# A rarely taken general path behind a fused transformer block: fewer engines in its conditional, another order of its blocks

## The chip, the cores and the metric

The kernel runs on one core of a Trainium2 chip. A core has five engines with an instruction queue each: TensorE (matrix products, written to PSUM), VectorE, ScalarE, GpSimd and SyncE; in the profile's lines they are PE (with PEld for its weight loads), DVE, ACT, POOL and SP. A letter q behind a name means the engine's queue itself (a branch, a semaphore, a DMA issue) and not its compute. Sixteen DMA engines move data between the chip's main memory and SBUF; they also bring the engines' instructions. Engines wait for each other by semaphores. The metric is the device time of one execution in microseconds (us); the time of a kernel is the median of its runs.

## The reference

One transformer block with conditioning: 2048 tokens of 512 values, 32 heads of 16, a gated feed-forward part of width 1376, inputs and output in bfloat16.

```python
mod = silu(c) @ w_mod                       # six vectors: sa, ca, ga, sb, cb, gb
h = layernorm(x) * (1 + ca) + sa
q, k, v = split(h @ wqkv)                   # 32 heads of 16
phi(y) = concat(softmax(y @ w_phi), softmax(-(y @ w_phi)))
kv = sum over tokens of phi(k)^T v;  z = sum over tokens of phi(k)
o = (phi(q) @ kv) / (phi(q) @ z + 1e-6)
x = x + ga * (o @ wo)
h = layernorm(x) * (1 + cb) + sb
x = x + gb * ((sigmoid(h @ w_gate) * (h @ w_up)) @ w_down)
```

The softmax runs over the 16 features of one head. Its maximum needs to be subtracted only where the exponent could overflow.

## The kernel before

**Tiling.** The 2048 tokens are 16 tiles of 128. For each tile the first part normalises, transposes and scales the input (`h1T`), multiplies it by the folded weights `wqk_f` (w_phi is multiplied into wqkv once at the start), takes the exponentials without subtracting a maximum, and sums `kvacc` over all tiles. The second part, `downstream`, works through the tiles in chunks of 1, 1, 2, 4, 4 and 4: queries, quotient, output projection, second normalisation, gate and up products (`g_ps`, `u_ps`, lines 854 to 859), gated product (lines 864 to 875), and the down product `y_ps` (line 895). A final addition on VectorE (line 905) makes the output tile `ot`, and SyncE stores it (line 907). The last chunk's last two tiles are stored in an order of their own, one of them in two halves of 256 columns, so that the very last store is 64 KB.

**Order.** All this work is entered as tasks in a graph `G` with durations, due times and buffers; a planner puts the tasks in an order, `emit` writes them out, and each engine runs its instructions in that order.

**Two paths.** Leaving out the maximum is safe only where the features are bounded. `bound_tasks` computes such a bound from the weights during the second part and writes `flag`, which is 0 when the bound holds. `load_flag` (lines 913 to 915) reads it into a register of each engine; it is called while the final addition of tile 12 is written out. After all tasks of `G`, line 1306 opens a conditional: if the flag is above 0, a second graph `G2` recomputes everything in the general way, with maxima and minima subtracted, and stores all 16 tiles again. With the inputs used here the flag is 0.

```python
with tc.If(fv_box[0] > 0, preferred_fallthrough_block=False):
    emit(order2)
```

Every engine whose register holds the flag has a test of its own at that place, and a skip part for when the general path doesn't run: it waits until the engine's own earlier work is done and adds to its semaphores what the general path would have added. Loads and stores go through eight semaphores, which SyncE issues DMAs on in turn, so SyncE's skip part has eight such instructions. With `preferred_fallthrough_block=False` the instructions behind the test are the skip part, and the general path is elsewhere.

**The closing.** At the end of the program (line 1333) SyncE waits for all semaphores, the five engines drain and report to GpSimd, GpSimd clears the semaphores, and a second round of reports ends the execution.

**What `G2` uses.** `features` computes the products on TensorE, maxima, minima, differences, sums, reciprocals and products on VectorE, and exponentials on ScalarE; the rest of `G2` is the same `downstream` as in the first graph, with VectorE for most of the element-wise work and SyncE for transposes and for 17 stores.

Of the kernel before, what the change touches and what calls it, by code (L numbers as in the profile page):

```python
# [9 lines left out]
FP32 = mybir.dt.float32  # L10
BF16 = mybir.dt.bfloat16
INT32 = mybir.dt.int32
ACT = mybir.ActivationFunctionType
ALU = mybir.AluOpType
AX = mybir.AxisListType

P = 128
S, D, H, DH, F = 2048, 512, 32, 16, 1376
NT = S // P
KT = D // P  # L20
FT = (F + P - 1) // P
F_LAST = F - (FT - 1) * P
NG = 8
VC = DH + 1
# [402 lines left out]
def kernel(  # L427
# [4 lines left out]
    nc = tc.nc  # L432
    pe, act, dve, pool, sp = nc.tensor, nc.scalar, nc.vector, nc.gpsimd, nc.sync

    ctx.enter_context(tc.manual_schedule())
    cst = ctx.enter_context(tc.tile_pool(name="cst", bufs=1))
    psp = ctx.enter_context(tc.tile_pool(name="psp", bufs=1, space=bass.MemoryType.PSUM))


    x_sb = cst.tile([P, NT, D], BF16, name="x_sb")  # L440
    wv_sb = cst.tile([P, KT, D], BF16, name="wv_sb")
    wqk_f = cst.tile([P, KT, 2 * D], BF16, name="wqk_f")
    wo_sb = cst.tile([P, KT, D], BF16, name="wo_sb")
    wg_sb = cst.tile([P, KT, F], BF16, name="wg_sb")
    wu_sb = cst.tile([P, KT, F], BF16, name="wu_sb")
    wd_sb = cst.tile([P, FT, D], BF16, name="wd_sb")
    wr_sb = cst.tile([P, KT, P], BF16, name="wr_sb")
    h1T = cst.tile([P, KT, S], BF16, name="h1T")
    kvbd = cst.tile([P, NG, P + 16], BF16, name="kvbd")
    ident = cst.tile([P, P], BF16, name="ident")  # L450
    bmask = cst.tile([P, P], BF16, name="bmask")
    mask4 = cst.tile([P, 4], BF16, name="mask4")
    modc = cst.tile([P, 16], FP32, name="modc")
    mhalf = cst.tile([P, NT], FP32, name="mhalf")
# [14 lines left out]
    flag = cst.tile([1, 1], INT32, name="flag")  # L469
# [14 lines left out]
    VS = 4  # L484
    vaug = [cst.tile([P, H, VC], BF16, name=f"vaug{i}") for i in range(VS)]
# [3 lines left out]
    o_v = out.flatten_outer_dims().rearrange("(n p) d -> p n d", p=P)  # L489
    wqkv_v = A_wqkv.rearrange("(j p) n -> p j n", p=P)  # L490
    wmod_v = w_mod.rearrange("(j p) n -> p j n", p=P)
    bm = bmask[:].rearrange("p (h f) -> p h f", f=DH)
# [19 lines left out]
    CAPS = {"bank": 8, "r2k": 6, "xn": 8, "x1": 9, "eT": 3, "h2": 2, "hm": 2, "tg": 2, "ot": 2, "smS": 2, "m": 2, "den": 2, "cc": 3, "ks": 3, "oT": 3, "vaug": VS}  # L512
# [13 lines left out]
    def bank(name, shape=None, dtype=FP32):  # L526
        return Buf("bank", shape or [P, 512], dtype, name)

    def small(name, shape):
        return Buf(name if name in CAPS else "ks", shape, FP32, name)  # L530

    def emit(order):
        for t in order:
            for b in t.bufs:
                if b.cls not in ("h2", "hm", "vaug"):
                    get(b)
            t.fn(t.eng)
# [4 lines left out]
    def kv_tasks(G, acc, t, ph, va, due, parts=((0, 8),), chain=()):  # L542
        for a, b in parts:
            def kv(e, a=a, b=b):
                for g in range(a, b):
                    pe.matmul(acc[g // 4][:, (g % 4) * HC:(g % 4 + 1) * HC], lhsT=ph[:, g * P:(g + 1) * P],  # L546
                              rhs=vaug[va.slot][:, 4 * g:4 * g + 4, :].rearrange("p h d -> p (h d)"),
                              start=(t == 0 and g % 4 == 0), stop=(t == NT - 1), skip_group_check=True)
            halves = [("kvacc", h) for h in range(2) if a < 4 * h + 4 and b > 4 * h]
            G.add(f"kv{t}.{a}", {"PE": 0.031 * (b - a)}, kv, r=[("phi", t, a), ("vaug", t)], w=[*halves, *chain],  # L550
                  bufs=[ph, va] + [acc[h] for _, h in halves], due=due)
# [359 lines left out]
    fv_box = []  # L911

    def load_flag():
        fv_box.append(nc.values_load(flag[0:1, 0:1], min_val=0, max_val=1,
                                     skip_runtime_bounds_check_because="written as 0 or 1"))

    def bound_tasks(G, due):
        for j in range(KT):
# [150 lines left out]
    for g, ts in enumerate(LG):  # L1069
        n = len(ts)  # L1070
        gd = T0 + ts[0] * KP + LGD[g]
# [17 lines left out]
        if nmr_used:  # L1089
            def f_nm(e, ts=ts):  # L1090
                for t in ts:
                    dve.tensor_scalar(nmr[:, 0, t:t + 1], mv1[:, t, 0:1], rs1[:, t:t + 1], -1.0, op0=ALU.mult, op1=ALU.mult)
            G.add(f"nmr1_{g}", {"DVE": 0.02 + 0.1 * n}, f_nm,
                  r=[("rs1", g)], w=[("nmr1", g)], due=gd)
        for t in ts:
            xn = Buf("xn", [P, D], BF16, "xn")
            xns.append(xn)

            def f_xn(e, t=t, xn=xn):
# [4 lines left out]
                else:  # L1104
# [3 lines left out]
                  bufs=[xn], due=gd, port=("POOL", "DVE"), pref=XN1[t] if t < 2 else [e for e in XN1[t] if e != "DVE"] or ["ACT"])  # L1108
        if TD[g]:
            for q, t in enumerate(ts):  # L1110
                G.add(f"xT1_{t}", {"SP": 1.22}, lambda e, t=t, xn=xns[q]: sp.dma_start_transpose(h1T[:, :, t * P:(t + 1) * P], xn[:]),
                      r=[("xn1", t)], w=[("h1raw", t)], bufs=[xns[q]], due=gd, nbytes=-1)
        for j in range(KT):
            dst = h1T[:, j, ts[0] * P:(ts[-1] + 1) * P]
# [24 lines left out]
    for t in range(NT):  # L1139
# [8 lines left out]
        def f_v(e, t=t, vp=vp):  # L1148
            for j in range(KT):
                pe.matmul(vp[:], lhsT=h1T[:, j, t * P:(t + 1) * P], rhs=wv_sb[:, j, :], start=(j == 0), stop=(j == KT - 1))  # L1150
# [6 lines left out]
        for a, b in parts:  # L1157
# [12 lines left out]
            w = (b - a) / 8.0  # L1170
# [65 lines left out]
    order = G.order()  # L1236
    emit(order)

    G2 = Graph(CAPS)

    def features(t, side, key):
        sv = "p (h s j) -> p s h j" if side else "p (s h j) -> p s h j"

        pk = bank("pk_g")

        def f1(e):
            for j in range(KT):
                pe.matmul(pk[:], lhsT=h1T[:, j, t * P:(t + 1) * P], rhs=wqk_f[:, j, side * D:(side + 1) * D], start=(j == 0), stop=(j == KT - 1))
        G2.add(f"gp{side}{t}", {"PE": 0.9}, f1, w=[("gp", side, t), "chain"], bufs=[pk])
        ext = small("ext", [P, 2, H])  # L1250
        dd = [Buf("r2k", [P, H, DH], FP32, "dd") for _ in range(2)]
        ph = Buf("r2k", [P, 2 * H * DH], BF16, "gphi")

        def f2(e):
            pv = pk[:].rearrange("p (h j) -> p h j", j=DH)
            dve.tensor_reduce(ext[:, 0], pv, axis=AX.X, op=ALU.max)
            dve.tensor_reduce(ext[:, 1], pv, axis=AX.X, op=ALU.min)
            for s in range(2):
                dve.tensor_tensor(dd[s][:], pv, ext[:, s].unsqueeze(2).to_broadcast([P, H, DH]), op=ALU.subtract)

        def f3(e):
            for s in range(2):
                act.activation(dd[s][:], dd[s][:], ACT.Exp, scale=1.0 - 2.0 * s)

        def f4(e):
            for s in range(2):
                dve.tensor_reduce(ext[:, s], dd[s][:], axis=AX.X, op=ALU.add)
            dve.reciprocal(ext[:], ext[:])
            for s in range(2):
                dve.tensor_tensor(ph[:].rearrange(sv, s=2, j=DH)[:, s], dd[s][:],  # L1270
                                  ext[:, s].unsqueeze(2).to_broadcast([P, H, DH]), op=ALU.mult)
        G2.add(f"gd{side}{t}", {"DVE": 2.8}, f2, r=[("gp", side, t)], w=[("gd", side, t), "chain"], bufs=[pk, ext] + dd + [ph])
        G2.add(f"ge{side}{t}", {"ACT": 1.2}, f3, r=[("gd", side, t)], w=[("ge", side, t), "chain"], bufs=dd)
        G2.add(f"gn{side}{t}", {"DVE": 2.8}, f4, r=[("ge", side, t)], w=[key, "chain"], bufs=[ext] + dd + [ph])
        return ph

    acc = [bank(f"gacc{i}") for i in range(2)]
    for t in range(NT):
        ph = features(t, 1, ("phi", t, 0))
        vp = bank("gv")  # L1280
        va = Buf("vaug", None, None, "gva")

        def f_v(e, t=t, vp=vp):
            for j in range(KT):
                pe.matmul(vp[:], lhsT=h1T[:, j, t * P:(t + 1) * P], rhs=wv_sb[:, j, :], start=(j == 0), stop=(j == KT - 1))
        G2.add(f"gV{t}", {"PE": 0.9}, f_v, w=[("v", t), "chain"], bufs=[vp], due=t)
        G2.add(f"gva{t}", {"ACT": 0.6}, lambda e, vp=vp, va=va: act.copy(vaug[va.slot][:, :, 0:DH], vp[:].rearrange("p (h d) -> p h d", d=DH)),
               r=[("v", t)], w=[("vaug", t), "chain"], bufs=[vp, va], due=t)
        kv_tasks(G2, acc, t, ph, va, t, chain=["chain"])
    kvbd_tasks(G2, acc)  # L1290
    eT2 = [Buf("eT", [P, NG, 512], BF16, f"geT{cq}") for cq in range(4)]
    for cq in range(4):
        for tl in range(4):
            t = 4 * cq + tl
            ph = features(t, 0, ("gphq", t))
            tp = bank("gtp", [P, NG, P], BF16)

            def f_t(e, ph=ph, tp=tp):
                for g in range(NG):
                    pe.transpose(tp[:, g, :], ph[:, g * P:(g + 1) * P], ident[:])  # L1300
            G2.add(f"gT{t}", {"PE": 0.5}, f_t, r=[("gphq", t)], w=[("gT", t), "chain"], bufs=[ph, tp], due=100.0 + t)
            G2.add(f"gTc{t}", {"ACT": 1.0}, lambda e, cq=cq, tl=tl, tp=tp: act.copy(eT2[cq][:, :, tl * P:(tl + 1) * P], tp[:]),
                   r=[("gT", t)], w=[("eT", cq, tl)], bufs=[tp, eT2[cq]], due=100.0 + t)
    downstream(G2, eT2, 200.0, False)
    order2 = G2.order()
    with tc.If(fv_box[0] > 0, preferred_fallthrough_block=False):
        emit(order2)


# [28 lines left out]
```

## Time and profile before

| what | us |
|---|---|
| median of three runs | 216.68 (216.2 to 217.49) |
| span of the profiled execution, first to last instruction | 215.3 |
| time of that execution itself | not listed beside its span |
| TensorE busy | 202.7 |
| VectorE busy | 166.1 |
| ScalarE busy | 113.0 |
| GpSimd busy | 101.3 |
| last matmul, end | 209.3 |
| last store, issue | 209.7 |

The profile comes from one execution; its times count from the first instruction. The page's table of engines counts compute only: branches, register loads, semaphores, drains and DMA issues are not in it and are seen by asking for their lines. The conditional is line 1306, the flag's loads are line 914, the closing is line 1333. In the DMA table the queue q1 carries the kernel's transfers and the queues q8 and q14, of the kind "instruction", carry instructions: q8 packets of 16 KB, q14 packets of 8 KB. A DMA share is a part of all 16 engines, so one engine at work is a share of 0.06.

### The profile page before, as it was taken

How to read it: one execution, taken by the hardware profiler on the slowest of the kernel's cores; microseconds unless marked ns; L12 is line 12 of the kernel's file. 1: busy time of each engine (PE TensorE's matmuls, PEld its weight loads, DVE VectorE, ACT ScalarE, POOL GpSimd, SP SyncE). 2: the span in 40 equal slices, each digit the busy share in tenths (PEclk: the TensorE clock that was granted, in tenths of full speed). 3: DMA queues.
4: the chain of work that ended last, by engine and by line, in shares of the span. 5: the costliest groups of instructions: out<-in, count | busy, mean ns of one | idle time of the engine just before them, and what ended most of it. 6: DMA issues, size and time to landing. Idle time of an engine off the chain costs nothing.

```text
span 215.3 us, 4319 instructions
## 1 busy us (share of the span) xinstructions
PE 202.7 (94%) x1512; PEld 113.4 (53%) x1539; DVE 166.1 (77%) x447; ACT 113.0 (53%) x278; POOL 101.3 (47%) x133
## 2 busy tenths in 40 slices
PE   7998998999999999989999999999999999999980
PEld 2744454555666577857964544454444444444450
DVE  3799999988689999859989978999899871237340
ACT  3699987998959894345442233643211651235000
POOL 3859999999969999511552222403205210000000
PEclk9999999999999999999999999999999999999996
DMA  6997997970000210250614110233201231000111
GB/s 183 371 255 167 372 193 164 411 246 0 0 3 0 52 26 5 59 90 1 99 24 72 27 28 7 68 73 74 52 14 37 52 73 50 0 0 0 55 50 34
DMA packets 31423, 18.76 MB, mean 87 GB/s; under 512 B 20673, under 2 KB 29346, under 8 KB 31394
## 3 DMA queue, kind: packets, MB, share of 16 engines
q1 hardware_dynamic: 30864, 18.39, 33.2%
q8 instruction: 14, 0.23, 0.4%
q14 instruction: 15, 0.12, 0.2%
q10 hardware_dynamic: 530, 0.02, 0.1%
HBM read 11.58 MB, written 2.10 MB: 64 GB/s over the span
## 4 chain that ended last, share of the span: by engine, by line
PE 70%; DVE 9%; DMA 8%; SPq 4%; issue 2%; ACT 2%; POOL 1%; DVEq 0%; POOLq 0%
PE y_ps L895 16%; PE u_ps L854 15%; PE g_ps L854 15%; PE a_ps L762 5%; PE v_ps L1150 4%; DMA wqk_sb<-in_A_wqkv_dram 4%; PE k_ps L1146 3%; PE q_ps L1224 3%; SPq L1044 3%; DVE u L735 2%; DMA oT<-o 2%; DMA x_sb<-in_A_x_dram 2%; PE num L645 2%; PE kvacc L546 2%; PE g_ps L856 1%
## 5 line engine op out<-in xcount | busy, mean ns | idle before, releaser
L864 ACT ACTIVATE tg<-g_ps 128x512 bf16<-128x512 f32 (+4 forms) x66 | 28.9, 453 | 57.7 <-PE g_ps L854 43.8
L875 DVE SCALAR_TENSOR_TENSOR wmod_sb<-tg,u_ps 128x512 bf16<-128x512 bf16 (+4 forms) x63 | 29.7, 494 | 17.3 <-PE u_ps L854 9.4
L895 PE MATMUL y_ps<-wd_sb,wmod_sb 128*128 128x512 bf16 (+3 forms) x178 | 41.3, 366 | 0.4
L753 POOL TENSOR_TENSOR o<-u 128x512 bf16<-128x512 f32 x14 | 17.7, 1268 | 32.0 <-DVE u L720 15.0
L1168 POOL TENSOR_TENSOR phi<-e,ks 128x1024 bf16<-128x1024 bf16 (+2 forms) x22 | 31.4, 1454 | 0.5 <-DVE ks L1178 0.3
L854 PEld LDWEIGHTS <-wg_sb 128*128 128x128 bf16 (+1 forms) x252 | 21.6, 99 | 16.2 <-issue 1.0
L854 PEld LDWEIGHTS <-wu_sb 128*128 128x128 bf16 (+1 forms) x252 | 21.8, 99 | 15.2
L895 PEld LDWEIGHTS <-wmod_sb 128*128 128x128 bf16 (+1 forms) x187 | 17.9, 98 | 16.4
L854 PE MATMUL u_ps<-wT_sb,wu_sb 128*128 128x512 bf16 (+2 forms) x123 | 23.3, 322 | 0.2
L854 PE MATMUL g_ps<-wT_sb,wg_sb 128*128 128x512 bf16 (+2 forms) x121 | 23.2, 321 | 0.1
L854 PE MATMUL g_ps<-wqk_sb,wg_sb 128*128 128x128 bf16 (+4 forms) x127 | 19.8, 287 | 0.5 <-DVE wqk_sb L828 0.4
L1165 DVE TENSOR_REDUCE ks<-e 128x64 f32<-128x1024 bf16 (+2 forms) x22 | 19.7, 906 | 0.6 <-ACT e L1162 0.6
L854 PE MATMUL u_ps<-wqk_sb,wu_sb 128*128 128x128 bf16 (+4 forms) x127 | 19.6, 287 | 0.1
L905 DVE TENSOR_TENSOR ot<-y_ps,x 128x512 bf16<-128x512 f32 (+1 forms) x17 | 11.2, 656 | 9.8 <-PE y_ps L895 9.8
L1162 ACT ACTIVATE e<-k_ps 128x512 bf16<-128x512 f32 (+2 forms) x44 | 18.3, 499 | 0.3 <-POOL phi L1168 0.3
L762 PE MATMUL a_ps<-wo_sb,oT 128*128 128x512 bf16 x62 | 16.3, 379 | 1.2 <-DMA oT<-o 1.0
L1229 ACT ACTIVATE eT<-q_ps 128x512 bf16<-128x512 f32 x32 | 16.8, 618 | 0.9 <-PE q_ps L1224 0.9
L1146 PE MATMUL k_ps<-wqk_f,h1T 128*128 128x512 bf16 x60 | 15.9, 379 | 1.1 <-ACT h1T L1126 0.8
L1150 PE MATMUL v_ps<-wv_sb,h1T 128*128 128x512 bf16 x63 | 15.8, 379 | 0.1
L1224 PE MATMUL q_ps<-h1T,wqk_f 128*128 128x512 bf16 x60 | 15.1, 378 | 0.1
L1075 DVE BATCH_NORM_STATS2 st<-x_sb 128x6 f32<-128x512 bf16 x16 | 10.8, 676 | 3.3 <-DMA x_sb<-in_A_x_dram 3.3
L767 DVE TENSOR_TENSOR x<-a_ps,x_sb 128x512 f32<-128x512 f32 x16 | 10.9, 684 | 2.5 <-PE a_ps L762 2.3
(154 smaller groups left out, 322.3 us busy)
## 6 DMA issues: line engine op xcount, KB each, us to landing
wmod_sb<-in_w_mod_dram SPq DMA_DIRECT2D x4, 512.0 KB, 6.5
out_dram<-ot SPq DMA_DIRECT2D x15, 128.0 KB, 1.7
x_sb<-in_A_x_dram SPq DMA_DIRECT2D x3, 512.0 KB, 7.5
wg_sb<-in_B_w_gate_dram SPq DMA_DIRECT2D x1, 1376.0 KB
wu_sb<-in_B_w_up_dram SPq DMA_DIRECT2D x1, 1376.0 KB, 9.4
wd_sb<-in_B_w_down_dram SPq DMA_DIRECT2D x1, 1280.0 KB, 12.2
wqk_sb<-in_A_wqkv_dram SPq DMA_DIRECT2D x2, 512.0 KB, 4.3
wmod_sb<-in_w_mod_dram SPq DMA_DIRECT2D x1, 1024.0 KB, 8.3
```

The lines of the kernel that those rows point to most:

```text
L753: G.add(f"o{t}", {"POOL": 1.3, "DVE": 0.62}, lambda e, ub=ub, o=o: engine(e).tensor_tensor(o[:], ub[0][:].rearrange("p h d -> p (h d)"), u ...
L762: pe.matmul(ap_[:], lhsT=oT[:, j, :], rhs=wo_sb[:, j, :], start=(j == 0), stop=(j == KT - 1))
L854: pe.matmul(ps[:fsz, 0:n], lhsT=w[:, j, ft * P:ft * P + fsz], rhs=h[:, j, 0:n], start=(j == 0), stop=(j == KT - 1))
L864: G.add(f"tg{k}.{ft}", {"ACT": 0.13 + n * 0.00083}, lambda e, tg=tg, g_ps=g_ps, fsz=fsz, n=n: act.activation(tg[:fsz, 0:n], g_ps[:fsz, 0:n ...
L875: dve.scalar_tensor_tensor(hm_all[:fsz, hm[k].slot, ft, 0:n], tg[:fsz, 0:n], 1.0, u_ps[:fsz, 0:n], op0=ALU.add, op1=ALU.mult)
L895: pe.matmul(y[:, 0:c1 - c0], lhsT=hm_all[:fsz, hm[k].slot, ft, tl * P:(tl + 1) * P], rhs=wd_sb[:fsz, ft, c0:c1], start=(ft == 0), stop=(ft ...
L1146: pe.matmul(kp[:], lhsT=h1T[:, j, t * P:(t + 1) * P], rhs=wqk_f[:, j, D:2 * D], start=(j == 0), stop=(j == KT - 1))
L1150: pe.matmul(vp[:], lhsT=h1T[:, j, t * P:(t + 1) * P], rhs=wv_sb[:, j, :], start=(j == 0), stop=(j == KT - 1))
L1162: act.activation(ee[:, ha:hb, s, :], kp[:, ha * DH:hb * DH].rearrange("p (h j) -> p h j", j=DH), ACT.Exp, scale=1.0 - 2.0 * s)
L1165: dve.tensor_reduce(ks[:, ha:hb].rearrange("p h s -> p (h s)"), ee[:, ha:hb].rearrange("p h s j -> p (h s) j"), axis=AX.X, op=ALU.add)
L1168: pool.tensor_tensor(ph[:, ha * 32:hb * 32].rearrange("p (h j) -> p h j", j=DH), ee[:, ha:hb].rearrange("p h s j -> p (h s) j"), ks[:, ha: ...
L1224: pe.matmul(qp[:], lhsT=wqk_f[:, j, blk * P:(blk + 1) * P], rhs=h1T[:, j, cq * 512:(cq + 1) * 512], start=(j == 0), stop=(j == KT - 1))
```

## The change

Three things change, and nothing in the tasks of the graph `G`.

1. The flag is loaded on TensorE, ScalarE and GpSimd only. VectorE and SyncE have no register with it and no conditional.
2. The general path is written anew, tile by tile, without a graph, for these three engines. What VectorE did goes to GpSimd: maxima, minima and sums by halving (`gen_fold`), reciprocals by a power (`gen_recip`), products and additions; ScalarE copies every PSUM result to SBUF first. Transposes are done by TensorE (`gen_transposed`). The results are gathered in `x_sb`, and one DMA, issued by GpSimd, stores all of them.
3. The conditional is opened without `preferred_fallthrough_block`.

```diff
     def load_flag():
-        fv_box.append(nc.values_load(flag[0:1, 0:1], min_val=0, max_val=1,
-                                     skip_runtime_bounds_check_because="written as 0 or 1"))
+        fv_box.append(nc.values_load(flag[0:1, 0:1], engines=[mybir.EngineType.PE, mybir.EngineType.Activation, mybir.EngineType.Pool],
+                                     min_val=0, max_val=1, skip_runtime_bounds_check_because="written as 0 or 1"))
...
-    G2 = Graph(CAPS)
-
-    def features(t, side, key):
...
+    def gen_fold(src, n, op, name):
+
+
+        r = src.shape[1]
+        t, d = gen_tile("r2k5", [P, r, n // 2], FP32, name), None
+        if op != ALU.add:
+            d = gen_tile("r2k4", [P, r, n // 2], FP32, name + "d")
+        while n > 1:
+            n //= 2
+            a, b = src[:, :, 0:n], src[:, :, n:2 * n]
+            if op == ALU.add:
+                pool.tensor_tensor(t[:, :, 0:n], a, b, op=ALU.add)
...
+    def gen_features(t, side):
+        pk = gen_bank(0)
+        for j in range(KT):
+            pe.matmul(pk[:], lhsT=h1T[:, j, t * P:(t + 1) * P], rhs=wqk_f[:, j, side * D:(side + 1) * D], start=(j == 0), stop=(j == KT - 1))
+        ps = gen_tile("x10", [P, H, DH], FP32, "g_pk")
+        act.copy(ps[:].rearrange("p h d -> p (h d)"), pk[:])
...
+    def gen_keys():
+        acc = [gen_bank(1 + i) for i in range(3)]
+        for t in range(NT):
+            ph = gen_features(t, 1)
...
+    def gen_tokens(t):
+        ph = gen_features(t, 0)
+        tp = gen_transposed(ph, NG, 1, "g_tp")
...
+        yo = gen_tile("x11", [P, D], FP32, "g_y")
+        act.copy(yo[:], y[:])
+        pool.tensor_tensor(x_sb[:, t, :], yo[:], x1[:], op=ALU.add)
...
-    downstream(G2, eT2, 200.0, False)
-    order2 = G2.order()
-    with tc.If(fv_box[0] > 0, preferred_fallthrough_block=False):
-        emit(order2)
+    with tc.If(fv_box[0] > 0):
+        gen_keys()
+        for t in range(NT):
+            gen_tokens(t)
+        pool.dma_start(o_v[:, :, :], x_sb[:])
```

## The prediction

> **What bounds the kernel now.** I read three things in order: the chain that ended last, to see where the compute stops; the instructions of the lines of the conditional and of the closing, which the page of busy engines leaves out; and the DMA after the last store.
>
> The chain over the last 20 us, with its start, its length and what it was:
>
> ```profile
> 198.63 5.19 PE y_ps L895 x24
> 203.81 0.05 issue
> 203.87 5.40 PE y_ps L895 x35
> 209.27 0.02 issue
> 209.29 0.42 DVE ot L905
> ```
>
> TensorE sets the pace up to 209.3, then one addition on VectorE ends at 209.71. The span is 215.3, so 5.6 us (2.6%) lie behind the last computed value. The general path does not run in this execution, since behind the conditional (line 1306) nothing follows but the closing (line 1333). What the queues do meanwhile, by line: instruction, count, duration in ns (min/median/max), first and last start.
>
> ```profile
> L1306 SPq EVENT_SEMAPHORE  x8: 17/17/17, 212.8 to 213.3; - x8
> L1306 ACTq COMPARE_BRANCH  x2: 38/44/49, 198.7 to 199.0; - x2
> L1306 PEldq COMPARE_BRANCH  x2: 95/1890/3686, 206.4 to 209.4; - x2
> L1306 DVEq COMPARE_BRANCH  x2: 51/53/55, 209.3 to 209.9; - x2
> L1306 SPq COMPARE_BRANCH  x2: 43/48/53, 210.1 to 213.4; - x2
> ...
> L1333 SPq EVENT_SEMAPHORE  x10: 17/28/28, 213.9 to 215.2; - x10
> L1333 ACTq DRAIN  x2: 8/44/80, 201.4 to 214.8; - x2
> L1333 DVEq DRAIN  x2: 10/34/58, 212.7 to 214.8; - x2
> L1333 PEldq DRAIN  x2: 8/40/73, 213.2 to 214.8; - x2
> ```
>
> Each engine has two branches: the test, not taken here, and a jump over the general path, which lies behind. TensorE's jump at 209.4 takes 3.69 us; ScalarE's closing begins 2.4 us after its jump at 199.0, VectorE's 2.8 us after its jump at 209.9. SyncE tests at 210.1, and its next instruction starts only at 212.8. These waits show whom it stood for, the first being the last store's landing:
>
> ```profile
> SPq L1306 <- SPq L1306: 2.7, 1, 2.7
> SPq L1333 <- PEq L1333: 0.6, 2, 0.5
> ```
>
> Why that landing is so late is in the DMA. First the stores' time from issue to landing; then four stretches behind the last issue (start:end, length, engines, granted clock, DMA share, GB/s); then the queues between 210.5 and 211.78:
>
> ```profile
> DMA to landing us min/median/max: 1.5/1.7/2.9
> ```
> ```profile
> 209.70:211.00 1.30, 0.00 (x0) 0.00 (x0) 0.02 (x1) 0.00 (x0) 0.00 (x0) 1.00 0.49 157
> 211.00:211.75 0.75, 0.00 (x0) 0.00 (x0) 0.00 (x0) 0.00 (x0) 0.00 (x0) 0.92 0.00 0
> 211.75:212.25 0.50, 0.00 (x0) 0.00 (x0) 0.00 (x0) 0.00 (x0) 0.00 (x0) 0.50 0.07 8
> ```
> ```profile
> q1 hardware_dynamic: 136, 0.06, 16.7%
> q8 instruction: 1, 0.02, 5.1%
> q14 instruction: 1, 0.01, 1.5%
> ```
>
> The last store is issued at 209.74 and its data moves by 211.0, except one sixteenth (a share of 0.07 of 16 engines) which moves between 211.75 and 212.25, after a pause. In the pause the one 16 KB instruction packet of q8 is in flight: it starts at 210.73 and takes 1.05 us, 1.3 us behind TensorE's jump. So I read it as TensorE fetching its jump target through the DMA engine that also carries that sixteenth. The landing comes at 212.81; 15 of its 16 parts had landed by 211.44.
>
> **The change, part by part.** The sum goes against this execution. Its span is 215.26 us; no other time of its own is listed. The median of the three runs, 216.68, is 1.42 above the span, and I keep those 1.42 for what lies around it.
>
> *Loads of the flag on VectorE and SyncE go.* They took 0.54 and 0.51 us at 200.2 and 201.3. VectorE's lies beside the addition of 200.18 to 200.87, SyncE's between two stores of which the second waits for data until 202.81. Gain 0; without that cover each would give its half microsecond once. The other three loads stay in place, TensorE's 0.49 us at 199.8 under matmuls without a gap.
>
> *VectorE's conditional goes:* two branches, one semaphore, 2.8 us up to its closing at 212.7. SyncE reached its own end only at 214.44, so this alone gives 0.
>
> *SyncE's conditional goes.* Behind the landing at 212.82 stand eight semaphore instructions (0.6 us), then a branch, and the closing's first wait is at 213.92: 1.10 us, all on the path. Nothing replaces it on SyncE, since the new general path issues nothing there. The gain is 1.10; it cannot be negative by any row, and it is at most that plus the closing's own eight waits (0.5 us, 213.92 to 214.44) should those have passed before the landing. I take 1.10, because the closing as it stands waits for this store's semaphore first.
>
> *The block order.* Before, the skip runs straight on, waits until its engine has done its own work and then jumps far. In the default order I expect the general path to follow the test and the skip to be the jump. TensorE's test is at 206.4, 2.9 us before its last matmul ends. If the far jump is taken there, its 3.69 us end at 210.1, and its closing starts about 210.3 rather than 213.2. The fetch, 1.3 us behind the jump, would occupy its DMA engine from 207.7 to 208.75. Stores there: the one issued at 206.16 has landed by 207.68, and the next, issued at 208.81, moves data from 209.64. So the last store lands in its undisturbed time, 209.74 plus 1.5 to 1.7, 211.25 to 211.45; I take 211.4, so 1.41 earlier than 212.81. At worst the gain is 0 (the jump stays behind the last matmul); no row gives more than 1.55. TensorE's next fetch came 4.6 us after the jump (214.04), which would now be 211.0, just behind the store's last packet at 210.93: close enough to matter below. VectorE's own small fetch at 210.87 disappears as well.
>
> *What is queued behind the jump:* on TensorE only its semaphore and the closing; 13 or so matmuls are before it and should already be queued. Nobody waits for that engine's closing before 212. ScalarE's jump (198.7) and GpSimd's (177.2) have 10 us and more of room; at 2.4 us each they hide.
>
> *The general path's new body and its one store on GpSimd's DMA.* It does not run, so its instructions cost nothing. What exists on the skip side is GpSimd's bookkeeping for a DMA that did not go: one more semaphore instruction (17 ns) at 177.3, hidden. In the closing one more wait may join SyncE's eight, 0.06 us. What a DMA queue of GpSimd costs a launch, the trace does not show. From below 0; from above the dearest thing on a queue other than TensorE's, ScalarE's 2.4 us between jump and closing. I take 0.06, the semaphore rows being nearest to what is added.
>
> Sum: landing 211.4, then the closing as before, 215.26 - 213.92 = 1.34, gives 212.75; with 0.06 still 212.8. That is 2.5 us less: 216.68 - 2.5 = 214.2.
>
> **The rivals.**
>
> *The jump stays late.* If a taken branch waits for the matmuls before it, or if the default order is the one there is, TensorE's fetch again lies over the last store. All taken branches in this trace stand behind their engine's own wait, so nothing shows one with work in flight; the tests not taken do run ahead (206.4, against the last matmul's end at 209.3). The same holds if the second fetch slides 0.1 us earlier into the store. Landing 212.81 + 1.34 = 214.15 (TensorE's closing at 213.2 still comes in time), a gain of 1.1: 215.6.
>
> *GpSimd's queue eats the gain.* With 2.4 us added behind the landing the span is 212.75 + 2.4 = 215.15: 216.6, no change. Against it: GpSimd's closing now consists of instructions of 0.03 to 0.14 us.
>
> *TensorE fetches twice (the slower side).* If the skip part and the closing lie too far apart, two far jumps follow each other. Place: behind the last matmul; price: a second 3.69 us. First jump 209.44 to 213.13, second to 216.8, then 0.1 of draining and 0.75 of the final barrier: 217.7, so 219.1. It decides from the point where both come after 209.3: if the first is at 206.4, the second ends at 213.8 and the time is 216.0. For it speaks that each far jump of TensorE shown here costs that much; against it, that VectorE's and SyncE's last branch reached the closing with one stall at most, and that two short parts next to each other fit one fetch. The Trainium skill, "Runtime: NRT & Kernel Launch", section "Instruction fetch mechanics", says that a taken branch to a place outside the two fetched pages stalls until that page is loaded; the 3.69 us row agrees, and by this rule the default order, which makes the skip the taken branch, can only cost, unless the other order jumps far too. Here it does.
>
> **How the numbers follow.** One execution against another differs by up to 1.3 us here (216.2 to 217.49), and about 0.5% (1.1 us, so 215.6) is what a measurement of this kernel can tell from no change. Chances: the forecast, 214.2, 0.60; the jump stays late, 215.6, 0.20, half of it on each side of the bound; GpSimd's queue, 216.6, 0.10; fetching twice, 219.1, 0.10. Faster 0.60 + 0.10 = 0.70, same 0.10 + 0.10 = 0.20, slower 0.10. The range reaches from the forecast with the closing's waits already passed (213.7) less 0.4 of scatter to the late jump plus 0.7 of scatter: 213.3 to 216.3, which leaves the twice-fetching and part of the GpSimd case out.
>
> **What the changed profile would show.** Right: no line of the conditional on VectorE and SyncE; TensorE's long branch starts at about 206.4 and its closing near 210.3; the 16 KB instruction packet ahead of the last store; that store lands in 1.5 to 1.7 us; SyncE's closing starts at 211.4 instead of 213.9; the chain up to 209.3 is the same. Wrong: a long branch at 209.4, a sixteenth of the last store behind the rest, a second long branch, or GpSimd as the last at the final barrier. A shift of the work before 209.3 is in none of these terms and would also break the number.

## The result, and the profile after

The changed kernel takes 215.72 us (median of 14 runs, 214.48 to 216.58) against 216.63 before (14 runs, 216.20 to 218.04): a ratio of 0.9943, 95% interval 0.9919 to 0.9966. So it is faster by 0.6%, about 1 us, where 2.5 us had been forecast. The profiled execution has a span of 214.3 us, 1.0 less than before, and a time of its own of 216.02; some 1.7 us lie around a span.

The compute did not change. The chain's last pieces (start, length, what):

```profile
198.49 5.19 PE y_ps L895 x24
203.68 0.05 issue
203.73 5.40 PE y_ps L895 x35
209.13 0.02 issue
209.16 0.42 DVE ot L905
```

The last addition ends at 209.58 instead of 209.71, which is scatter. Next, the lines of the conditional (1380 now) and of the closing (1410 now): count, durations in ns, first and last start.

```profile
L1380 POOLq EVENT_SEMAPHORE  x1: 17/17/17, 179.9 to 179.9; - x1
L1380 POOLq INC_SWDGE_SEM  x1: 160/160/160, 180.0 to 180.0; - x1
L1380 ACTq COMPARE_BRANCH  x1: 50/50/50, 198.6 to 198.6; - x1
...
L1380 PEldq COMPARE_BRANCH  x1: 3478/3478/3478, 206.3 to 206.3; - x1
L1380 PEldq EVENT_SEMAPHORE  x1: 51/51/51, 209.8 to 209.8; - x1
```
```profile
L1410 SPq EVENT_SEMAPHORE  x10: 17/28/28, 212.9 to 214.2; - x10
...
L1410 DVEq DRAIN  x2: 19/242/464, 209.2 to 213.7; - x2
L1410 PEldq DRAIN  x2: 8/8/8, 209.9 to 213.7; - x2
```

Most of what was announced is there. VectorE and SyncE have no line of the conditional. Each remaining engine has one branch instead of two, TensorE's long one starts at 206.3, three microseconds earlier than before, and TensorE is in its closing at 209.9 instead of 213.2. SyncE goes from the landing straight into its closing. But that closing starts at 212.9, not at 211.4. Whom SyncE waited for (us in total, times, longest):

```profile
SPq L1410 <- DMA out_dram<-ot: 2.9, 1, 2.9
SPq L1410 <- PEq L1410: 0.8, 2, 0.6
```

The last store is late again. The stretches behind its issue (DMA share and GB/s are the last two columns), and the queues between 210.4 and 211.78:

```profile
209.60:210.80 1.20, 0.00 (x0) 0.00 (x0) 0.00 (x0) 0.00 (x0) 0.00 (x0) 1.00 0.50 154
210.80:211.75 0.95, 0.00 (x0) 0.00 (x0) 0.00 (x0) 0.00 (x0) 0.00 (x0) 1.00 0.00 0
211.75:212.25 0.50, 0.00 (x0) 0.00 (x0) 0.00 (x0) 0.00 (x0) 0.00 (x0) 1.00 0.07 8
```
```profile
q1 hardware_dynamic: 136, 0.06, 15.4%
q8 instruction: 1, 0.02, 5.8%
```

It is the old picture with another fetch. The trace has two 16 KB packets here; I read the first as the jump's target and the second as the block behind it. The first runs from 207.30 to 208.37, between two stores. Then TensorE resumes at 209.74, and 0.77 us later the second is on its way: from 210.50, for 1.29 us. A sixteenth of the last store, nine of its 144 packets, moves only at 211.78, as that packet ends.

The span's 0.97 us are made of: compute 0.14 earlier; the last store's way from issue to landing 3.23 us instead of 3.07, so 0.17 lost; from the landing to the end 1.45 us instead of 2.45, so 1.00 won. So in these two executions the gain is SyncE's missing skip part and jump.

### The profile page after: what moved, and what is told of

The parts are those of the page before. It is cut to its first block, busy times and chain, and to the rows that moved or that the text cites. A ratio compares the mean times of both kernels' runs of the same rounds, so it can differ in the third digit from the quotient of the medians.

```text
span 214.3 us, 4302 instructions
## 1 busy us (share of the span) xinstructions
PE 201.7 (94%) x1512; PEld 112.6 (53%) x1539; DVE 166.0 (77%) x447; ACT 113.0 (53%) x278; POOL 101.1 (47%) x133
## 4 chain that ended last, share of the span: by engine, by line
PE 68%; DVE 11%; DMA 10%; SPq 4%; issue 2%; POOL 1%; ACT 1%; DVEq 0%; POOLq 0%; ACTq 0%
PE y_ps L895 16%; PE u_ps L854 16%; PE g_ps L854 15%; PE a_ps L762 5%; DMA wqk_sb<-in_A_wqkv_dram 4%; PE q_ps L1224 3%; PE v_ps L1150 3%; SPq L1044 3%; PE k_ps L1146 2%; DVE u L735 2%; DMA oT<-o 2%; DMA h1T<-xn 2%; DMA x_sb<-in_A_x_dram 2%; PE num L645 2%; DVE ks L1165 2%
```

## The experiments

Two questions were open: whether the fetch makes the store late or only stands beside it, and what each of the three parts of the change is worth. In the rows of the experiments, ratios are against the kernel before on the same chip; its medians there were 217.38 (old order, five engines, no conditional, four matmuls), 216.90 (order alone; two, six and eight matmuls) and 216.72 (the last row), so kernels are compared by their ratios. "Fetch" is the start of TensorE's 16 KB packet nearest to the last store, "landing" the store's landing, both in us after that store's issue, from the packets and semaphores in the trace of the one profiled execution.

| kernel | median us | ratio (95% interval) | fetch | landing |
|---|---|---|---|---|
| before | 216.63 | 1 | 0.99 | 3.07 |
| changed | 215.72 | 0.9943 (0.9919 to 0.9966) | 0.90 | 3.23 |
| changed, old order | 215.71 | 0.9927 (0.9902 to 0.9952) | 0.68 | 2.78 |
| changed, flag on five engines | 216.12 | 0.9950 (0.9918 to 0.9981) | 1.01 | 3.32 |
| before, new order | 216.66 | 0.9976 (0.9954 to 0.9998) | 1.00 | 3.64 |
| changed, no conditional | 213.89 | 0.9839 (0.9802 to 0.9877) | none | 1.53 |
| changed, 2 spare matmuls | 214.05 | 0.9886 (0.9852 to 0.9919) | 1.67 | 1.53 |
| changed, 4 spare matmuls | 214.48 | 0.9882 (0.9838 to 0.9927) | 1.81 | 1.54 |
| changed, 6 spare matmuls | 214.50 | 0.9901 (0.9870 to 0.9931) | 2.12 | 1.54 |
| changed, 8 spare matmuls | 214.62 | 0.9899 (0.9872 to 0.9926) | 2.55 | 1.98 |
| changed, old order, 2 spare matmuls | 216.29 | 0.9963 (0.9936 to 0.9990) | 1.42 | 3.51 |

### The block order undone

```diff
-    with tc.If(fv_box[0] > 0):
+    with tc.If(fv_box[0] > 0, preferred_fallthrough_block=False):
```

> The new kernel with the blocks in the old order. Theory: the order alone moves the branch and nothing at the end. TensorE's long branch goes back to about 209.3, its closing to about 213.0; its fetch, 1.3 us behind the branch, lies over the last store again, which lands near 212.7 as it does with the new order. Time as the new kernel's, 215.7 (215.3 to 216.1). Rival (the order brought the gain of 1 us and SyncE's missing conditional nothing): 216.6, as before the change.

Measured: 215.71, as the changed kernel. TensorE has its two branches again, the long one at the end:

```profile
L1380 PEldq COMPARE_BRANCH  x2: 95/1750/3406, 206.4 to 209.4; - x2
L1380 PEldq EVENT_SEMAPHORE  x1: 51/51/51, 209.3 to 209.3; - x1
```

Its closing begins at 212.9 and the store lands at 212.5, both 0.1 to 0.2 us from what was expected. In the changed kernel the order is worth nothing that can be measured; the other two parts, the loads and the new general path, bring the gain.

### The order alone, on the kernel before

```diff
-    with tc.If(fv_box[0] > 0, preferred_fallthrough_block=False):
+    with tc.If(fv_box[0] > 0):
```

> The kernel before with the default block order and nothing else: all five engines keep their conditional and the old general path. Theory: TensorE jumps at 206.4; SyncE now jumps far right behind its last issue (210.1), some 2.5 us, ends at 212.7, beside the landing of the last store, which TensorE's second fetch still delays to 212.8; then eight semaphores, and the closing follows without another jump: 0.4 us less than before. Rival (the order is worth the whole gain): 1.0 us less. Rival (the order is worth nothing): same as before.

Measured: a ratio of 0.9976, so about 0.5 us less, near the theory's 0.4 and below the rival's 1.0; its interval only just excludes no change. SyncE's lines show what it does to the closing:

```profile
L1306 SPq EVENT_SEMAPHORE  x8: 17/17/17, 213.1 to 213.6; - x8
...
L1306 SPq COMPARE_BRANCH  x1: 53/53/53, 209.8 to 209.8; - x1
```

One branch instead of two: the half microsecond between SyncE's second branch and its closing is gone, the eight semaphores behind the landing stay. The landing is later than before in the profiled execution (3.64 us against 3.07), which takes the half microsecond back there, so the profile does not show the gain of the ratio.

### The flag on all five engines

```diff
-        fv_box.append(nc.values_load(flag[0:1, 0:1], engines=[mybir.EngineType.PE, mybir.EngineType.Activation, mybir.EngineType.Pool],
-                                     min_val=0, max_val=1, skip_runtime_bounds_check_because="written as 0 or 1"))
+        fv_box.append(nc.values_load(flag[0:1, 0:1], min_val=0, max_val=1, skip_runtime_bounds_check_because="written as 0 or 1"))
```

> The new kernel with the flag loaded on all five engines, so that VectorE and SyncE have a register with it. Theory: what cost SyncE 1.1 us was a skip part of eight semaphores and a jump over the old general path behind the landing; the new general path has nothing on SyncE, so a test there has nothing to wait for and lies in the shadow of the last store's landing: 215.7 (215.4 to 216.2). Rival (the test itself costs the microsecond): 216.7.

Measured: 216.12, inside the theory's range, with a ratio beside the changed kernel's. The rival's 216.7 would be 0.997 here, which the interval does not exclude, so the time alone decides little. The lines decide more:

```profile
L1379 DVEq COMPARE_BRANCH  x1: 72/72/72, 209.5 to 209.5; - x1
...
L1379 SPq COMPARE_BRANCH  x1: 53/53/53, 210.3 to 210.3; - x1
```
```profile
SPq L1409 <- DMA out_dram<-ot: 2.7, 1, 2.7
SPq L1409 <- PEq L1409: 0.8, 2, 0.6
```

SyncE has its test, 53 ns, and no skip semaphores; it then waits 2.7 us for the landing. A test in that shadow is hidden. What cost a microsecond was the skip part of a path on which SyncE had work. The new general path was not run by itself, with five loads and the old order; that it brings the gain follows from this run and the one before it together.

### The conditional left out

```diff
-    with tc.If(fv_box[0] > 0):
-        gen_keys()
-        for t in range(NT):
-            gen_tokens(t)
-        pool.dma_start(o_v[:, :, :], x_sb[:])
```

> The new kernel with the conditional and the general path left out; the output is the same where the bound holds. Theory: no jump, so no far fetch beside the last store; it lands 1.5 to 1.7 us after its issue, near 211.2, SyncE's closing starts there, the span ends near 212.7, 214.1 in time, 1.6 less than the new kernel. Rival (the last sixteenth is late for a reason of its own, whatever TensorE fetches): landing still near 212.8, time 215.7.

Measured: 213.89. This is no replacement, as it lacks the general path, but it is the floor: 1.6% below the kernel before. The stretches around and behind its last issue, at 209.86, and the queues from 209.8 to 212.5:

```profile
209.80:210.65 0.85, 0.00 (x0) 0.00 (x0) 0.04 (x1) 0.00 (x0) 0.00 (x0) 1.00 0.43 146
210.65:211.10 0.45, 0.00 (x0) 0.00 (x0) 0.00 (x0) 0.00 (x0) 0.00 (x0) 1.00 0.50 146
211.10:212.50 1.40, 0.00 (x0) 0.00 (x0) 0.00 (x0) 0.00 (x0) 0.00 (x0) 1.00 0.00 0
```
```profile
q1 hardware_dynamic: 281, 0.19, 21.8%
```

No instruction packet, no straggling sixteenth: all 144 packets of the last store are through by 211.05, and it lands 1.53 us after its issue. The closing is shorter as well, 1.16 us from landing to end where the changed kernel has 1.45, so the 1.6% are not all the landing's.

### Spare matmuls ahead of the test

This moves the fetch and leaves it in. Matmuls that nobody reads stand behind the last real one; the test, and with it both fetches, comes later by their length, and the last addition and the last store do not depend on them.

```diff
+    tail_ps = psp.tile([P, 512], FP32, name="tail_ps", tag=f"bank0", bufs=1)
+    for _ in range(4):
+        pe.matmul(tail_ps[:], lhsT=wd_sb[:, 0, 0:P], rhs=wd_sb[:, 0, :], start=True, stop=True)
     with tc.If(fv_box[0] > 0):
```

> The new kernel with four more 128x512 matmuls on TensorE behind the last one and ahead of its test; nobody reads them. Theory: test and jump come four matmuls (0.87 us) later, at 207.1; the second 16 KB fetch starts near 211.4 instead of 210.50, behind the last store's data; that store lands near 211.2 and the time is 214.2 although TensorE does more work. Rival (the last sixteenth is late anyway): 215.7.

> Two spare matmuls behind the last one: TensorE's second fetch should start 1.3 us after the last store's issue (it was 0.9 in the new kernel, 1.0 in the one with five engines, 1.8 with four matmuls). Other engines' data of that store moves from 0.83 to 1.19 us after the issue. Theory: at 1.3 the fetch is behind the data, the landing takes 1.5 to 1.7 us and the time is the four-matmul kernel's, 214.5 (214.0 to 215.2). If the DMA engine takes the store's sixteenth later than the others do, the fetch still comes first: landing 3.5 us after the issue, 216.

> Six spare matmuls: second fetch 2.2 us after the last store's issue. Theory: clear of the store; TensorE's closing at about 210.8 relative to a last addition at 208.7, still ahead of SyncE's: 214.3 (213.8 to 215.0). Rival (the extra work itself moves the end): 0.43 us more than with four, 214.9.

> Eight spare matmuls: second fetch 2.6 us after the last store's issue, TensorE's closing about 2.5 us after it, SyncE's closing waits end 2.05 us after it: so TensorE becomes the last at the final barrier by some 0.4 us. Theory: 214.7 (214.2 to 215.4); between four and six matmuls the time is lowest. Rival (the landing is late for its own reason): 216 and more.

Measured: 214.48 with four, 214.05 with two, 214.50 with six, 214.62 with eight. More work on TensorE makes the kernel faster: ratios of 0.9882 to 0.9901 where the changed kernel has 0.9943, some 1 us. The nearest pair on one chip is the old order, 215.71, and four matmuls, 214.48. With two, TensorE's branch, SyncE's waits and the last store's stretches:

```profile
L1384 PEldq COMPARE_BRANCH  x1: 3818/3818/3818, 206.4 to 206.4; - x1
```
```profile
SPq L1414 <- DMA out_dram<-ot: 1.2, 1, 1.2
SPq L1414 <- PEq L1414: 0.8, 2, 0.6
```
```profile
209.30:210.15 0.85, 0.00 (x0) 0.00 (x0) 0.02 (x1) 0.00 (x0) 0.00 (x0) 1.00 0.41 140
210.15:210.55 0.40, 0.00 (x0) 0.00 (x0) 0.00 (x0) 0.00 (x0) 0.00 (x0) 1.00 0.56 164
210.55:211.00 0.45, 0.00 (x0) 0.00 (x0) 0.00 (x0) 0.00 (x0) 0.00 (x0) 1.00 0.00 0
211.00:212.30 1.30, 0.00 (x0) 0.00 (x0) 0.00 (x0) 0.00 (x0) 0.00 (x0) 1.00 0.06 13
```

SyncE's wait for the store falls from 2.9 to 1.2 us; the store's data is complete by 210.55, and the 16 KB fetch, alone in the last stretch (a share of 0.06), starts at 211.02. It came later than I had worked out, 1.67 us behind the issue and not 1.3, because the jump itself took 3.82 us here and not 3.48. So the case that I meant to try was not tried, and that two matmuls suffice in this execution is partly luck.

With eight I had expected TensorE to be the last at the final barrier. It wasn't: its closing starts at 211.5, SyncE is done with its waits at 211.9. What shows instead, in the stores issued from 208.3 on (the landing is of the first of the two, which alone is matched to its issue), is

```profile
L907 SPq DMA_DIRECT2D out_dram<-ot x2: 332/556/781, 208.5 to 209.4; - x2
DMA to landing us min/median/max: 2.5/2.5/2.5
```

The first fetch, at 208.75, now falls on the store issued at 208.50; part of it lands 2.5 us after its issue. The last store's own issue then takes 781 ns instead of 332, all its packets move 0.45 us later, and it lands after 1.98; why the issue takes longer these runs do not show, the busy queue being the nearest reading. In the profile there is a price on both sides of the gap. In the times none shows: two to eight spare matmuls cannot be told apart by these intervals.

### The same matmuls where they move the fetch to no use

```diff
-    with tc.If(fv_box[0] > 0):
+    tail_ps = psp.tile([P, 512], FP32, name="tail_ps", tag=f"bank0", bufs=1)
+    for _ in range(2):
+        pe.matmul(tail_ps[:], lhsT=wd_sb[:, 0, 0:P], rhs=wd_sb[:, 0, :], start=True, stop=True)
+    with tc.If(fv_box[0] > 0, preferred_fallthrough_block=False):
```

> The new kernel in the old block order, with two spare matmuls behind the last one. There TensorE jumps only when its own work is done, which is 0.43 us later than without them. Theory (what the spare matmuls do is to move a fetch): TensorE's closing now starts near 213.3 and SyncE's, by whether the fetch at 1.1 us behind the issue still catches the store's sixteenth, at 211.3 or 212.9; the end is bound by one of the two at 214.2 to 214.4 either way: 215.9 (215.4 to 216.4), no gain from the matmuls. Rival (busy TensorE by itself makes the end faster, its clock for instance): 214.1 as with two matmuls in the new order.

Measured: 216.29, no gain. In its profile:

```profile
L1384 PEldq COMPARE_BRANCH  x2: 95/1900/3706, 206.4 to 209.4; - x2
```
```profile
SPq L1414 <- DMA out_dram<-ot: 3.2, 1, 3.2
SPq L1414 <- PEq L1414: 0.8, 2, 0.6
```

TensorE's granted clock from 211 to 212 is 1.00 with two spare matmuls in either order (0.62 in the old order without them), and the time falls only where the fetch leaves the store. In this order TensorE's own closing starts only at 213.2, which would hide an earlier landing from the time; but the landing isn't earlier, it comes after 3.51 us. So a busy TensorE does not explain the gain.

## Why the prediction was right or wrong

The direction was right and the range holds the time, because it took in the first rival; the forecast value, 214.2, was not what came. What came is the first rival, 215.6, and there its second clause, that the second fetch lies over the store.

- **The bound at the end** (the last 5.6 us wait for one sixteenth of a store that a fetch delays): shown, as far as the landing goes. Without a fetch the store lands in 1.53 us; with it moved 1.7 us or more behind the issue, in 1.53 to 1.54 (two to six matmuls).
- **Flag loads on VectorE and SyncE, VectorE's conditional:** put at 0. The compute up to 209.6 is unchanged, and the kernel with five loads differs by less than its interval; nothing speaks against it.
- **SyncE's conditional**, put at 1.10 us: right, 1.00 from landing to end.
- **The block order**, put at 1.41 us: this is the step that failed. Its mechanism was half right: the jump is taken at 206.3 with matmuls still running, TensorE's closing comes at 209.9, and the first fetch passes between the stores. The term came out at -0.17. I had set the second fetch 4.6 us behind the jump, at 211.0, from the one such distance in the old trace, where the jump took 3.69 and the rest 0.91. Here the jump took 3.48 and the rest 0.77: 210.50. I had also taken the last packet of the store's other fifteen parts, 210.93, as the point from which a fetch no longer hurts. The runs put that point later: a fetch recorded 1.42 us behind the issue still went ahead of the sixteenth, when the other fifteen parts had been through by 1.18; at 1.67 it did not. A margin of 0.07 us, between two numbers of one execution, should not have been given 0.60 against 0.20. The jump itself sorts the runs better than its packet: in the six late landings TensorE jumped (old order) or resumed (new order) between 0.30 us before and 0.22 us after the last store's issue, in the four with spare matmuls in the new order 0.90 to 1.77 us after it, and the store's data starts 0.83 us after its issue (1.28 with eight). No run lies between 0.22 and 0.90, so this order is seen and its cause not shown.
- **GpSimd's bookkeeping**, put at 17 ns and hidden: its test and skip part cost about 3 us at 177 to 180, among them 160 ns for the DMA that did not run; hidden as said. The closing gained no semaphore instruction.
- **GpSimd's queue eats the gain:** no sign of 2.4 us. From SyncE's first closing wait to the end it takes 1.43 us, against the 1.34 assumed.
- **TensorE fetches twice, in series:** it does fetch twice, but the second block is fetched while TensorE already runs on; there is one stall. The rule of the Trainium skill, "Runtime: NRT & Kernel Launch", section "Instruction fetch mechanics", that a taken branch out of the two fetched pages stalls, agrees with every run with a conditional (3.4 to 3.8 us on TensorE). The same section of the Trainium skill says that the sequencer fetches the next page of instructions while it executes the current one; the second packet, 0.77 us after TensorE resumes, agrees. What decided here is where that packet falls.
- **The 1.42 us around the span:** this gap paired a median with another execution's span; 1.7 belongs to one execution. The difference does not depend on it.

## What to carry to other kernels

When a kernel ends in a store, look at what else uses the DMA engines in the last microseconds, and count instruction fetches among it: TensorE's jump at the end brought two here, read as its target and the block behind. Keep the work of an engine that ends late out of a rarely taken path: what cost SyncE a microsecond was its skip part, while its bare test was hidden. Place the jump of an engine that must have it so that neither fetch meets the last store. Here two matmuls that nobody reads do that in the profiled execution, at 0.9886 of the time before (0.9852 to 0.9919) against 0.9943 (0.9919 to 0.9966) for the change alone; the two were not timed side by side.

## What the runs showed of the hardware

- TensorE's taken branch does not wait for its work in flight: it jumped at 206.26 and its matmuls went on to 209.1.
- A second 16 KB packet, read as the block behind the jump's target, follows a jump without another branch: in the new order it starts 0.77 to 0.83 us after TensorE resumes, and it takes 1.1 to 1.6 us.
- One 16 KB packet holds back a sixteenth of a concurrent store: in all six late executions that sixteenth starts to move 0.01 to 0.02 us before the packet's recorded end (2.17 and 2.18 us after the issue in the changed kernel). The store then lands 2.8 to 3.6 us after its issue instead of 1.5, also when the record shows the packet starting after the other fifteen parts are done (1.42 against 1.18). That packet and sixteenth share a DMA engine is inferred from this, since the views don't name the engine; whether it is the same one each time is open.
- The runs of one kernel differ by 1.5 to 2.8 us (two spare matmuls: four runs of 213.7 to 214.1, two of 215.1 and 215.2), without a conditional by 1.0 and with eight spare matmuls by 0.4. Whether a fetch meets a store in some of those executions is open; only one of each was profiled, the fastest of its six with four and with six spare matmuls. The changed kernel's fastest runs, 214.48 and 214.52, lie near the forecast, so the loss in the block order need not be there in every execution. The general path itself ran in none of them, so what its new form costs when taken is not known.
